# A two-layer spectral filter and token mixer: a list of the filter's steps put in another order, two loads issued later, a first step that takes its products in another order, and four matmuls that nothing reads

## Chip, cores and metric

One core of one Trainium2 chip. The metric is the device time of one launch in microseconds. The kernel before takes 997.96 us as the median of three runs (997.35 to 1001.58); its one profiled execution took 999.61 us.

## What is computed

The input x has 2048 tokens (S) of 640 channels (D), in fp32. Two layers alternate, each with a layer norm ahead of it and a residual sum behind it, and the pair runs twice:

```
def _A_ref(x, w_r, w_i):
    X = rfft2(x, axes=(-2, -1)) * (w_r + 1j * w_i)
    return irfft2(X, s=(S, D), axes=(-2, -1))

def _B_ref(x, w1, b1, w2, b2):          # token mixer, F = 1728
    u = gelu(einsum("bsd,sf->bdf", _layernorm(x), w1) + b1)
    return transpose(einsum("bdf,fs->bds", u, w2) + b2)

x = x + _A_ref(_layernorm(x), w_r, w_i)
x = x + _B_ref(_layernorm(x), w1, b1, w2, b2)
# ... and the same two lines once more
```

## The kernel before

**Number format.** Almost every matmul operand is an fp32 value carried as two fp16 tiles, a high part (names ending in h) and a low part (ending in l). A product of two such values is three matmuls: high by high, high by low, low by high (`mm3`, `prods`). Each intermediate is evicted from PSUM by a pair of instructions: ACT writes the high part, then DVE writes what is left as the low part.

**The filter layer.** The transform over 2048 tokens is done as 128 x 16, so there are 16 rows j of 128 tokens. In the row part (`a0_...`) each row is normalised, folded over the channels into f, and multiplied by a table tM into `s1h`/`s1l`. In the first layer that is done with fp32 f straight from x. In the second layer it is done while the token mixer before it ends, except for the last row j = 15, which `a0_tail` takes by itself: 11 matmuls that nothing reads (`WARM`) keep PE at work while DVE, POOL and ACT normalise the row (tiles eo, ft0, ft1, then fht and flt). Then come the row's products (from fht and flt into two PSUM tiles) and their eviction: s1h on ACT, s1l on DVE.

The middle part is `a1`. It goes over 16 groups g of frequencies, each in these steps:

- `d` (`dstage`, PE): products of s1h and s1l with the table tD into a PSUM tile. Groups 0 and 1 take 48 matmuls each (8 places in the PSUM tile, of 6 terms each: s1h twice and s1l once from one part, and the same from another). Groups from 2 take three terms for each place from s1h and s1l directly, and a fourth from `stk`, a tile that `stack` gathers for two groups at a time out of a DRAM copy (`rest`) of s1h and s1l: five DMAs of 64 or 0.5 KB for each pair of groups.
- `ph`, `pl`: eviction by ACT (high) and DVE (low).
- `sA`, `sB` (PE): the two halves of the next transform, from ph and pl with the table tS2. Here `acted` and `follow` add a synchronisation by hand: the last matmul of sA is waited for by an ACT instruction, and the first of sB waits for that ACT instruction. In the kernel before it is the first ACT step that stands behind sA in the list.
- `ta`, `tb` (DVE): the PSUM result times the filter's real and imaginary weight, both from the tile w of that group.
- `sa`, `sb` (POOL): the sums of these products. `xh` (ACT) and `xl` (POOL) split them, `uh` and `ul` (ACT) copy some columns.
- `i` (PE) and `Yh`, `Yl` (ACT, DVE): the transform back over one axis and its eviction.

**What sets the order.** `a1` runs these steps from a list, `STEPS`, written as text and the same for both layers. Every engine executes its instructions in the order in which they were issued in the program, so the list fixes each engine's own order. Besides, the list decides where DMA issues fall. After each op, `a1` tests whether ta and tb of group g-3 are already issued; if so it issues the load of w of group g (`wload`, 321 KB, three buffers), and likewise `stack` for the next pair of groups once the d steps of the pair three earlier are issued. Both go to the SP queue, which issues in order: an issue that must wait for a buffer to be released holds all issues behind it. SP also brings the token mixer's weights (`raw`, 512 KB) for the stage that comes later. POOL issues three DMAs of the first stk, and two larger loads for the part behind `a1`: `tDi` (966 KB) and `tIM0` (512 KB), both after sb3.

In the first layer `also` hangs further ACT and DVE work between the steps (finding scales and splitting the first block of the mixer's weights, tiles raw, junk and wh). It hangs on named ops, so it moves when they move in the list.

All of DVE's, ACT's, PE's and POOL's arithmetic is recorded through one helper, so its line is 69 for all of it (70 in the changed kernel). Lines of their own have the DMA issues: 494 and 496 stk, 506 w, 654 tDi, 655 tIM0, 895 raw.

Of the kernel before, what the change touches and what calls it, by code (L numbers as in the profile page):

```python
# [24 lines left out]
FIRST = 2  # L25
WARM = 11
STEPS = '''
    d1@1 sA0@2 ph1 pl1 sB0 d2@0 sA1@1 ph2 tb0 d3@3 ph3 sB1 ta0 sa0 pl2 sb0 xh0 xl0 sA2@0 tb1 uh0 pl3 d4@2 ta1 sa1 sb1
    sB2 ph4 ta2 sA3@3 d5@1 ul0 pl4 tb2 sB3 sb2 ph5 pl5 sA4@2 xh1 sa2 d6@0 d7@1 ta3 ph6 tb3 sB4 pl6 tb4 xl1 uh1 ph7
    sA5@3 xh2 i0@0 sb3 sB5 pl7 sa3 ta4 ul1 Yh0 Yl0 tb5 sA6@1 xl2 xh3 ta5 sb4 d8@2 ph8 d9@0 sa4 xl3 xh4 sB6 uh3 ul3 sa5  # L30
    pl8 tb6 sA7@3 uh2 sb5 i1@2 ph9 sB7 Yh1 xl4 ta6 pl9 d10@1 xh5 sb6 xl5 sA8@0 sa6 Yl1 ul2 ta7 ph10 i3@2 tb7 sB8 Yh3
    pl10 sA9@3 i2@1 ta8 uh4 sa7 xh6 ul5 tb8 sB9 Yl3 d11@0 ul4 sb7 Yh2 Yl2 xh7 xl6 uh6 sb8 sa8 uh5 sA10@2 tb9 ph11 xl7
    ta9 pl11 d12@1 xh8 sB10 sa9 ph12 sb9 i4@3 Yh4 i5@0 ta10 tb10 pl12 xh9 Yh5 xl8 d13@2 Yl4 sb10 ph13 sA11@1 ul6 Yl5
    uh8 pl13 sA12@3 sB11 sa10 ul7 xl9 xh10 xl10 sB12 ta11 tb11 ta12 sA13@2 d14@0 ph14 ul8 sa11 i6@1 sb11 ul9 Yh6 uh7
    sB13 tb12 pl14 Yl6 d15@3 xh11 sa12 uh9 sA14@0 tb13 sb12 ph15 xl11 i7@1 sB14 ta13 pl15 uh10 i8@2 ul10 uh11 xh12
    sa13 Yh7 sb13 i9@3 ul11 xh13 uh13 tb14 ta14 xl12 Yl7 sa14 uh12 Yh9 sA15@0 Yh8 sb14 Yl9 xh14 xl13 i10@1 sB15 i11@3
    Yh10 ul13 Yl8 xl14 i13@2 Yh11 uh14 tb15a ta15a ul14 ul12 sb15a Yh13 tb15b sa15a ta15b Yl10 Yl11 i14@0 Yl13 xh15a
    sb15b i12@1 sa15b xl15a xh15b uh15 xl15b i15a@2 Yh14 Yh12 Yl14 Yl12 ul15 Yh15a i15b@3 Yh15b Yl15a Yl15b
'''
SEQ = [t + 7 * i for t in (6, 0, 1, 2, 3, 4, 5) for i in range(2)]  # L40
EPS = 1e-5
# [35 lines left out]
class Layers:  # L77
# [367 lines left out]
    def a1(self, first):  # L445
# [68 lines left out]

        def dstage(g, ps):
            part = lambda t: tuple(s[:, t * 16 + g].rearrange("p h a b -> p (h a b)") for s in (self.s1h, self.s1l))
            for c, bk, o0, o1, k in CL:
# [19 lines left out]
        def xhi(g, c, x):  # L537

            return T.activation(xs[g % NX][0][:, :, c], x, AF.Copy)
# [74 lines left out]
        dst, half, waiting = {}, {}, []  # L614
# [13 lines left out]
        def acted(ins):  # L628

            for g in waiting:  # L630
                follow(ins, half[g])
                half[g] = ins
            waiting.clear()

        def do(op):

            name, g, c, dve, k = re.fullmatch(r"([a-zABY]+)(\d+)([ab]?)(!?)(?:@(\d))?", op).groups()
            g, W, ps = int(g), V if dve else G, slots[int(k or 0)]
            pair = lambda: (tt[g][0], tt[g][1])
            if name == "d":  # L640
                dst[g] = psplit(dstage(g, ps))
            elif name == "ph":
                acted(next(dst[g]))
            elif name == "pl":
                pp[g] = next(dst.pop(g))
            elif name in ("ta", "tb"):
                term(g, name == "tb", part[c])
            elif name == "sa":
                suma(pair(), part[c], W)
            elif name == "sb":  # L650
                ins = sumb(pair(), part[c], W)
                if g == 3:
                    with self.after(ins):
                        nc.gpsimd.dma_start(self.tDi, A["tDi"])
                        nc.gpsimd.dma_start(self.tIM0, A["tIM"][:, 0:4])
            elif name == "xh":
                acted(xhi(g, part[c], tt[g][0][:, :, part[c]]))
            elif name == "xl":
                xlo(g, part[c], tt[g][0][:, :, part[c]], W)
            elif name in ("uh", "ul"):  # L660
                acted(twice(g, name == "ul"))
            elif name == "sA":
                ps2[g] = ps
                half[g] = s2half(g, ps, pp[g], 0)[1]
                waiting.append(g)
            elif name == "sB":
                follow(s2half(g, ps2[g], pp.pop(g), 1)[0], half.pop(g))
            elif name == "i":
                pv[g, c] = ps
                for lt in range(3)[ltile[c]]:  # L670
                    is2mm(ps, g, lt)
            elif name == "Yh":
                acted(yhi(g, pv[g, c], ltile[c]))
            elif name == "Yl":
                ylo(g, pv[g, c], ltile[c])

# [37 lines left out]
        for op in STEPS.split():  # L714
            do(op)
            if first:
                also(op)
            ended.add(op.split("@")[0])
# [1305 lines left out]
```

## Time and profile before

| what | us |
|---|---|
| timed runs, median (lowest, highest) | 997.96 (997.35, 1001.58) |
| profiled execution, its own time | 999.61 |
| its span in the trace | 997.8 |
| time around the span (999.61 - 997.8) | 1.8 |
| PE busy | 949.3 (95%) |
| DVE busy | 774.9 (78%) |
| ACT busy | 575.1 (58%) |
| POOL busy | 302.1 (30%) |
| first filter's `a1` | 60.2 to about 124.7 |
| last row (`a0_tail`) before the second filter | about 548 to 555 |
| second filter's `a1` | 554.6 to about 622.5 |

Times in the trace are microseconds from the start of the span. PE's busy time includes matmuls that run at a lower granted clock, so a busy PE isn't always at the same speed; the row of granted clock (PEclk) has to be read beside it. A view by windows gives, for a stretch of time, PE's busy time with the number of instructions, the granted clock as a share of the full one, the DMA engines' busy share and GB/s.

### The profile page before, as it was taken

What the parts mean: (1) busy time and instruction counts of PE and PEld (TensorE: products, weight loads), DVE (VectorE), ACT (ScalarE), POOL (GpSimd) and SP (SyncE); (2) the same over time, 40 slices, a digit from 0 to 9 for tenths busy, and PEclk for the clock granted to TensorE, in tenths of its full rate; (3) what the DMA queues carried; (4) which work ended last, traced back from release to release, by engine and by line L of the source; (5) the groups of instructions that cost most, each with busy time, mean ns of one, the idle gap of its engine ahead of it and who ended that gap; (6) DMA issues with size and microseconds to landing.
All of it is one profiled execution on the core that took longest, in us unless ns stands there. A gap on an engine that the chain in (4) does not pass through costs nothing.

```text
span 997.8 us, 22816 instructions
## 1 busy us (share of the span) xinstructions
PE 949.3 (95%) x9126; PEld 703.5 (71%) x9126; DVE 774.9 (78%) x1488; ACT 575.1 (58%) x888; POOL 302.1 (30%) x512
## 2 busy tenths in 40 slices
PE   3879999999999999999999888999999999999998
PEld 2767777677776777777777666776777777677776
DVE  7979989988677884666666779789955666998885
ACT  4857859698656565555544457684644445454431
POOL 6939857322112102222222388583000000000000
PEclk9589999999999999999999999999999999999999
DMA  7856357657667655464431564574555447655411
GB/s 231 279 176 205 98 196 240 221 211 271 216 231 238 207 161 201 127 215 127 129 107 51 174 190 130 166 235 167 169 169 159 138 143 258 218 173 196 146 48 51
DMA packets 67454, 176.30 MB, mean 177 GB/s; under 512 B 8122, under 2 KB 15444, under 8 KB 67348
## 3 DMA queue, kind: packets, MB, share of 16 engines
q1 hardware_dynamic: 59380, 146.39, 46.2%
q0 software_dynamic: 7968, 28.46, 7.6%
q8 instruction: 71, 1.16, 0.5%
q14 instruction: 35, 0.29, 0.1%
HBM read 127.24 MB, written 47.58 MB: 175 GB/s over the span
## 4 chain that ended last, share of the span: by engine, by line
PE 61%; DVE 14%; issue 10%; DMA 5%; ACT 5%; POOL 4%; SPq 0%; POOLq 0%; DVEq 0%; ACTq 0%
PE ps L69 61%; DVE st L69 2%; DVE f L69 2%; DVE xt L69 1%; DMA w1S<-sp 1%; DVE s1l L69 1%; DMA raw<-w2z 1%; DVE hl L69 1%; DMA xt<-x 1%; POOL xt L69 1%; DVE Yl L69 1%; DVE wl L69 1%; DMA w<-w 1%; POOL w1A L935 1%; DVE S L69 1%
## 5 line engine op out<-in xcount | busy, mean ns | idle before, releaser
L69 PEld LDWEIGHTS <-wh 128*128 128x128 f16 x2602 | 251.5, 98 | 101.0 <-issue 2.4
L69 PEld LDWEIGHTS <-wl 128*128 128x128 f16 x1610 | 157.4, 98 | 63.2 <-DVE wl L69 1.3
L69 PE MATMUL ps<-ul,wh 128*128 128x320 f16 x448 | 133.0, 299 | 0.0
L69 PE MATMUL ps<-uh,wl 128*128 128x320 f16 x448 | 133.1, 299 | 0.0
L69 PE MATMUL ps<-uh,wh 128*128 128x320 f16 x416 | 124.3, 299 | 0.0
L69 PE MATMUL ps<-hl,wh 128*128 128x320 f16 x496 | 102.2, 299 | 0.8 <-DVE hl L69 0.8
L69 PEld LDWEIGHTS <-wo 128*128 128x128 f16 x756 | 73.9, 98 | 29.4 <-DVE wo L69 0.8
L69 DVE SCALAR_TENSOR_TENSOR wl<-raw,s,wh 128x896 f16<-128x896 f32 (+2 forms) x63 | 73.8, 1175 | 23.7 <-ACT wh L69 21.7
L69 POOL TENSOR_TENSOR r<-v,mh 128x1 f32<-128x1 f32 x64 | 37.3, 583 | 158.4 <-DVE nm L69 148.8
L69 ACT ACTIVATE junk<-raw 128x896 bf16<-128x896 f32 (+1 forms) x60 | 59.5, 992 | 32.0 <-DMA raw<-w 28.8
L69 PE MATMUL ps<-tDi,Yh 128*128 128x322 f16 x320 | 71.3, 300 | 0.4 <-ACT Yh L69 0.3
L69 ACT ACTIVATE wh<-raw,s 128x896 f16<-128x896 f32 (+2 forms) x66 | 66.5, 1032 | 5.5 <-DVE s L69 4.9
L69 DVE TENSOR_TENSOR f<-eo 128x256 f32<-128x256 f32 (+1 forms) x124 | 39.0, 367 | 37.8 <-POOL eo L69 37.0
L69 POOL TENSOR_TENSOR xt<-xt,ec 128x320 f32<-128x320 f32 x64 | 53.2, 853 | 32.7 <-DVE xt L69 32.6
L69 ACT ACTIVATE z<-xt,nb,r 128x640 f32<-128x640 f32 x31 | 28.5, 919 | 54.2 <-POOL z L69 43.1
L69 PE MATMUL ps<-u,wo 128*128 128x320 f16 x420 | 59.0, 299 | 0.5 <-DVE wo L69 0.5
L69 DVE BATCH_NORM_STATS2 st<-xt 128x6 f32<-128x320 f32 x126 | 55.2, 479 | 5.3 <-DMA xt<-x 4.7
L69 PE MATMUL ps<-hha,wh 128*128 128x320 f16 x288 | 58.1, 299 | 0.9 <-DVE wh L69 0.9
L69 PE MATMUL ps<-tM,f 128*128 128x128 f32 x160 | 37.6, 402 | 21.7 <-DVE f L69 21.6
L69 POOL TENSOR_TENSOR eo<-z 128x320 f32<-128x320 f32 x60 | 52.2, 891 | 17.2 <-ACT z L69 15.2
L69 PE MATMUL ps<-tDi,Yl 128*128 128x322 f16 x192 | 55.7, 299 | 1.4 <-DVE Yl L69 1.4
L69 PE MATMUL ps<-hha,wl 128*128 128x320 f16 x256 | 53.4, 299 | 1.0 <-DVE wl L69 1.0
(254 smaller groups left out, 2335.5 us busy)
## 6 DMA issues: line engine op xcount, KB each, us to landing
xt<-x SPq DMA_DIRECT2D x79, 320.0 KB
raw<-w SPq DMA_DIRECT2D x32, 512.0 KB
w<-w SPq DMA_DIRECT2D x48, 321.0 KB
x<-xt SPq DMA_DIRECT2D x47, 320.0 KB
raw<-w SPq DMA_DIRECT2D x32, 448.0 KB
raw<-w2z SPq DMA_DIRECT2D x32, 448.0 KB
w1S<-sp POOLq DMA_DIRECT2D x20, 512.0 KB, 3.9
out<-xt SPq DMA_DIRECT2D x15, 320.0 KB
```

Of the source, the lines that this page charges most:

```text
L69: i = f(*a, **k)
L935: (self.nc.sync if k else self.nc.gpsimd).dma_start(st[:, i], w[i][:, c * q:c * q + q])
```

## The change

Five edits:

1. `STEPS` is written in another order. Each engine's own sequence of the list's steps is unchanged on PE, ACT, DVE and POOL, and so are the pairs of sA and the ACT step that waits for it, which the list now names itself (`ph1&0`: ph1 waits for sA0). What moves is everything that the list triggers by where an op stands: the loads on SP, and the extra ACT work of the first layer.
2. `tDi` is loaded in two halves, after sb7 and after sb9, and `tIM0` after sb11, instead of both after sb3.
3. `dstage(0)` issues the products of s1h for all eight places first (32 matmuls), then those of s1l (16). The start and stop flags follow. This holds for both layers.
4. In `a0_tail`, so before the second filter alone, two matmuls of 128x512 that nothing reads stand behind the first two products of fht, and two more behind the row's last product. They write a PSUM half that nothing reads.
5. `mm3` is written out in `a0_tail` for edit 4; the products themselves stay.

The diff, cut:

```
 STEPS = '''
-    d1@1 sA0@2 ph1 pl1 sB0 d2@0 sA1@1 ph2 tb0 d3@3 ph3 sB1 ta0 sa0 pl2 sb0 xh0 xl0 sA2@0 tb1 uh0 pl3 d4@2 ta1 sa1 sb1
...
+    d1@1 sA0@2 ph1&0 pl1 sB0 d2@0 tb0 ta0 sA1@1 d3@3 ph2&1 sa0 sb0 pl2 sB1 ph3 sA2@0 tb1 xh0 d4@2 uh0&2 pl3 xl0 ta1
...
+        def fill(n):
+            for _ in range(n):
+                self.PE.matmul(warm[:, 1], m[:, 0, 0], self.tD.rearrange("p a b -> p (a b)")[:, :512], start=True, stop=True)
...
-                self.mm3(q[:, c], (fh[:, c], fl[:, c]), (m[:, j % 4, 0], m[:, j % 4, 1]), True, True)
+                a, b = (fh[:, c], fl[:, c]), m[:, j % 4]
+                self.PE.matmul(q[:, c], a[0], b[:, 0], start=True, stop=False)
+                self.PE.matmul(q[:, c], a[0], b[:, 1], start=False, stop=False)
+                if not i and not o:
+                    fill(2)
+                self.PE.matmul(q[:, c], a[1], b[:, 0], start=False, stop=True)
             qs.append((q.rearrange("p (a h b) -> p a h b", h=2, b=4), slice(64 * i, 64 * i + n // 8)))
+        fill(2)
...
-                for i, (a, b) in enumerate(terms):
-                    for o, f in zip(HALF, HALF[::-1] if bk else HALF):
-                        mm(ps[o, bk, o0:o1], a[:, f], b, start=i == 0, stop=i == len(terms) - 1)
+                todo.append((bk, o0, o1, terms))
+            whole = [(slice(0, 6),)] if g else [(slice(0, 2), slice(3, 5)), (slice(2, 3), slice(5, 6))]
+            for cut in whole:
+                for bk, o0, o1, terms in todo:
+                    some = sum((terms[c] for c in cut), [])
+                    for i, (a, b) in enumerate(some):
+                        for o, f in zip(HALF, HALF[::-1] if bk else HALF):
+                            mm(
+                                ps[o, bk, o0:o1], a[:, f], b, start=cut is whole[0] and i == 0 and (g > 0 or o0 == 0),
+                                stop=cut is whole[-1] and i == len(some) - 1 and (g > 0 or o0 > 0),
+                            )
...
-                if g == 3:
+                if g in (7, 9, 11):
                     with self.after(ins):
-                        nc.gpsimd.dma_start(self.tDi, A["tDi"])
-                        nc.gpsimd.dma_start(self.tIM0, A["tIM"][:, 0:4])
+                        if g < 11:
+                            nc.gpsimd.dma_start(self.tDi[:, g // 9], A["tDi"][:, g // 9])
+                        else:
+                            nc.gpsimd.dma_start(self.tIM0, A["tIM"][:, 0:4])
```

Three places in the engines' order show what moves. The first is SP's queue in the second filter, before. In it w_1094 is the load of group 5, w_1102 that of group 6, w_1107 of group 7 and w_1110 of group 8; stk_1097 is the gathered tile of groups 12 and 13.

```order
L506 DMA w_1094_8776<-w 128x642
L494 DMA stk_1097_8873<-rest0_12_1063_8375 32x4x256
L496 DMA stk_1097_8873<-rest0_12_1063_8375 1x256
L494 DMA stk_1097_8873<-rest0_12_1063_8375 32x4x256
L494 DMA stk_1097_8873<-rest1_12_1063_8376 32x4x256
L496 DMA stk_1097_8873<-rest1_12_1063_8376 1x256
L506 DMA w_1102_8886<-w 128x642
L506 DMA w_1107_8976<-w 128x642
L506 DMA w_1110_9000<-w 128x642
```

And the same stretch in the changed kernel, where stk_1098 is the tile of groups 12 and 13, w_1113 the load of group 8, and raw_1179 a block of the mixer's weights:

```order
L518 DMA w_1094_8793<-w 128x642
L518 DMA w_1102_8892<-w 128x642
L506 DMA stk_1098_8880<-rest0_12_1063_8380 32x4x256
L508 DMA stk_1098_8880<-rest0_12_1063_8380 1x256
L506 DMA stk_1098_8880<-rest0_12_1063_8380 32x4x256
L506 DMA stk_1098_8880<-rest1_12_1063_8381 32x4x256
L508 DMA stk_1098_8880<-rest1_12_1063_8381 1x256
L518 DMA w_1107_8981<-w 128x642
L916 DMA raw_1179_10421<-w1 128x1024
L518 DMA w_1113_9078<-w 128x642
```

The load of group 6 has moved ahead of the five DMAs of stk; the load of raw_1179, which stood some rows further ahead (in front of the tile of groups 10 and 11), now stands behind the load of group 7.

The second place is PE at the end of `a0_tail` and the start of d0 of the second filter. Before, the row's last product (flt1) is followed by d0, which goes from four products of s1h to two of s1l in each place of the PSUM tile:

```order
L69 LDWEIGHTS flt1_1059_8317
L69 MATMUL ps1060_8333<-tM3_708_5780,flt1_1059_8317 128x128
L69 LDWEIGHTS s1h707_5769
L69 MATMUL ps1070_8395<-tD707_5771,s1h707_5769 64x160
...
L69 LDWEIGHTS s1l707_5770
L69 MATMUL ps1070_8395<-tD707_5771,s1l707_5770 64x160
```

In the changed kernel two of the unread matmuls (into ps1048, from tD and tM3) stand between the row's last product and d0, and d0 goes on with s1h:

```order
L70 LDWEIGHTS flt1_1059_8318
L70 MATMUL ps1060_8336<-tM3_708_5781,flt1_1059_8318 128x128
L70 LDWEIGHTS tM3_708_5781
L70 MATMUL ps1048_8283<-tD707_5772,tM3_708_5781 128x512
...
L70 LDWEIGHTS s1h707_5770
L70 MATMUL ps1070_8400<-tD707_5772,s1h707_5770 64x160
...
L70 MATMUL ps1070_8400<-tD707_5772,s1h707_5770 64x161
```

The first product of s1l stands behind 32 products of s1h now, and behind 4 before.

The third place is POOL in the first filter, before (the second filter's order is the same). The rows of ta are the sums sa and sb, from the products ta and tb; ta_255 is group 3:

```order
L69 TENSOR_TENSOR xl1_219_881<-ta_244_1231,xh1_219_880 128x2x321
L69 TENSOR_TENSOR ta_255_1411<-tb_258_1416,ta_255_1411 128x321
L654 DMA tDi218_874<-tDi 128x3864
L655 DMA tIM0218_873<-tIM 128x1024
L69 TENSOR_TENSOR ta_255_1411<-ta_255_1411,tb_258_1416 128x321
L69 TENSOR_TENSOR xl2_219_883<-ta_248_1252,xh2_219_882 128x2x321
```

In the changed kernel, where ta_282 is group 7 and ta_295 group 9:

```order
L70 TENSOR_TENSOR ta_282_1764<-tb_285_1807,ta_282_1764 128x321
L675 DMA tDi218_874<-tDi 128x1932
L70 TENSOR_TENSOR xl1_219_881<-ta_280_1697,xh1_219_880 128x2x321
...
L70 TENSOR_TENSOR ta_295_2004<-tb_292_1964,ta_295_2004 128x321
L675 DMA tDi218_874<-tDi 128x1932
L70 TENSOR_TENSOR xl3_219_885<-ta_288_1842,xh3_219_884 128x2x321
```

POOL's two issues behind the sums of group 3 are gone, and three issues stand behind those of groups 7, 9 and 11 (the last one, of tIM0, is not in these rows).

More of the change, by code (lines that the diff above doesn't have):

```diff
@@ new lines @@
+    tb7 sa6 sB8 pl10 Yh3 sA9@3 sa7 ta8 i2@1 uh4&9 sb7 xh6 tb8 ul5 sB9 ul4 xl6 Yl3 Yh2 d11@0 xh7 Yl2 sb8 uh6 sA10@2 uh5
+    tb9 sa8 d12@1 ph11&10 xl7 ta9 xh8 sB10 pl11 ph12 i4@3 sa9 ta10 sb9 i5@0 tb10 Yh4 xl8 pl12 xh9 d13@2 Yh5 Yl4 sb10
+    sA11@1 ph13 Yl5 sa10 sA12@3 ul6&11 xl9 uh8 pl13 sB11 ul7&12 xh10 sB12 ta11 sA13@2 xl10 d14@0 tb11 ta12 sa11 i6@1
+    ph14&13 tb12 sb11 ul8 ul9 sB13 pl14 Yh6 sa12 d15@3 uh7 sb12 Yl6 xh11 uh9 sA14@0 tb13 xl11 i7@1 ph15&14 ta13 uh10
+    ul10 sB14 pl15 uh11 xh12 sa13 i8@2 tb14 Yh7 sb13 i9@3 ta14 ul11 xl12 xh13 Yl7 uh13 sA15@0 uh12 Yh9 sa14 i10@1
@@ L39 @@
+    Yh8&15 sb14 Yl9 xl13 xh14 sB15 Yl8 i11@3 Yh10 tb15a xl14 ul13 ta15a i13@2 Yh11 tb15b uh14 sb15a ta15b ul14 Yl10
+    ul12 i14@0 Yh13 sa15a sb15b Yl11 xh15a sa15b i12@1 xh15b uh15 xl15a Yl13 Yh14 Yh12 Yl14 xl15b i15a@2 ul15 Yl12
+    i15b@3 Yh15a Yh15b Yl15a Yl15b
 '''
@@ L613, in a1 @@
         slots = [self.big() for _ in range(4)]
-        dst, half, waiting = {}, {}, []
+        dst, half = {}, {}
         tt = collections.defaultdict(dict)
@@ L626, in a1, with acted @@
             V.scalar_tensor_tensor(c, a, sc, b, op0=ALU.mult, op1=ALU.subtract)
-        def acted(ins):
-            for g in waiting:
+        def acted(ins, gs):
+            for g in map(int, gs.split(",") if gs else ()):
                 follow(ins, half[g])
                 half[g] = ins
-            waiting.clear()
         def do(op):
-            name, g, c, dve, k = re.fullmatch(r"([a-zABY]+)(\d+)([ab]?)(!?)(?:@(\d))?", op).groups()
+            name, g, c, dve, k, f = re.fullmatch(r"([a-zABY]+)(\d+)([ab]?)(!?)(?:@(\d))?(?:&([\d,]+))?", op).groups()
             g, W, ps = int(g), V if dve else G, slots[int(k or 0)]
@@ L642, in do @@
             elif name == "ph":
-                acted(next(dst[g]))
+                acted(next(dst[g]), f)
             elif name == "pl":
@@ L651, in do @@
                 ins = sumb(pair(), part[c], W)
-                if g == 3:
+                if g in (7, 9, 11):
                     with self.after(ins):
-                        nc.gpsimd.dma_start(self.tDi, A["tDi"])
-                        nc.gpsimd.dma_start(self.tIM0, A["tIM"][:, 0:4])
+                        if g < 11:
+                            nc.gpsimd.dma_start(self.tDi[:, g // 9], A["tDi"][:, g // 9])
+                        else:
+                            nc.gpsimd.dma_start(self.tIM0, A["tIM"][:, 0:4])
             elif name == "xh":
-                acted(xhi(g, part[c], tt[g][0][:, :, part[c]]))
+                acted(xhi(g, part[c], tt[g][0][:, :, part[c]]), f)
             elif name == "xl":
@@ L660, in do @@
             elif name in ("uh", "ul"):
-                acted(twice(g, name == "ul"))
+                acted(twice(g, name == "ul"), f)
             elif name == "sA":
@@ L717, in a1 @@
                 also(op)
-            ended.add(op.split("@")[0])
+            ended.add(re.match(r"\w+", op).group())
             if wn < NG and {f"ta{wn - 3}", f"tb{wn - 3}"} <= ended:
```

17 lines of the change are left out of this document (5 added, 12 removed).

## The prediction, made before the changed kernel ran

> **What bounds the kernel now.** I read the page first: the busy shares and the span in 40 slices.
>
> ```profile
> PE 949.3 (95%) x9126; PEld 703.5 (71%) x9126; DVE 774.9 (78%) x1488; ACT 575.1 (58%) x888; POOL 302.1 (30%) x512
> PE   3879999999999999999999888999999999999998
> ```
>
> PE is busy for 95% of the span, so the kernel can gain only where PE waits or runs slowly. A slice is 24.9 us. Slices 22 to 24 (548 to 623 us) show 8 in the PE row: this is the second filter. The first filter lies in slices 2 to 4. The change touches nothing outside these two stretches, so I read only them, next along the chain of work that ended last:
>
> ```profile
> 576.92 7.30 DMA w<-w
> ...
> 584.34 0.20 DVE tb L69
> ...
> 586.07 14.04 PE ps L69 x344
> ```
>
> A filter weight w is issued at 576.92 and lands 7.30 us later, and everything waits for it. DVE's own rows show what the wait costs (the bracket is idle time before the row, with its releaser):
>
> ```profile
> 572.97 0.88 DVE L69 SCALAR_TENSOR_TENSOR tb<-ps,sx,w 128x642 f32<-128x642 f32 x1
> ...
> 579.48 0.82 DVE L69 SCALAR_TENSOR_TENSOR pl<-ps,ph 128x642 f16<-128x642 f32 x1
> 584.34 0.89 DVE L69 SCALAR_TENSOR_TENSOR tb<-ps,sx,w 128x642 f32<-128x642 f32 x1 [4.04 <-DMA w<-w]
> ...
> 587.60 0.88 DVE L69 SCALAR_TENSOR_TENSOR ta<-ps,sx,w 128x642 f32<-128x642 f32 x1
> ...
> 590.37 0.83 DVE L69 SCALAR_TENSOR_TENSOR pl<-ps,ph 128x642 f16<-128x642 f32 x1 [1.11 <-ACT ph L69]
> ```
>
> DVE had finished pl of group 8 at 579.48 + 0.82 = 580.30 and stood until 584.34 for group 6's weight. Then the view by windows, cut to PE's clock steps (columns: stretch, its length and PE's busy time in it with the number of instructions, granted clock, DMA share, GB/s):
>
> ```profile
> 551.94:555.35 3.41, 1.82 (x21) 0.99 0.00 0
> 555.35:558.76 3.41, 3.26 (x50) 0.51 0.89 284
> ...
> 579.24:582.66 3.42, 2.82 (x78) 1.00 1.13 350
> 582.66:586.07 3.41, 0.00 (x0) 0.99 0.62 191
> 586.07:589.48 3.41, 3.41 (x50) 0.51 0.36 101
> ```
>
> The wait costs twice. PE does nothing from 582.66 to 586.07, and in the next 3.41 us its granted clock is 0.51. The same pair stands at 551.94 and 555.35: a window with PE busy for 1.82 of 3.41, then one at half the clock. In the first filter it is 2.03, and near the second filter's end 2.17, which is not followed by a slow one:
>
> ```profile
> 53.59:57.01 3.42, 2.03 (x13) 0.99 0.76 198
> 57.01:60.42 3.41, 2.62 (x14) 0.50 0.77 257
> ...
> 609.96:613.38 3.42, 2.17 (x65) 1.00 0.69 257
> 613.38:616.79 3.41, 3.41 (x109) 1.00 0.03 9
> ```
>
> So in this trace a window of 3.41 us with PE busy up to 2.03 us is followed by one at half the clock, and with 2.17 it is not.
>
> **A, the stall at 582 us.** SP's rows say why the weight was late:
>
> ```profile
> 572.63 0.35 SPq L506 DMA_DIRECT2D w<-w  x1
> 573.75 0.30 SPq L494 DMA_DIRECT2D stk<-rest  x1
> ...
> 576.92 3.00 SPq L506 DMA_DIRECT2D w<-w  x3
> ```
>
> Group 5's weight goes out at 572.63, then five stk issues come, the first waiting until 573.75, and only at 576.92 group 6's. By then the two loads that POOL issues are in flight ahead of it:
>
> ```profile
> 574.76 0.57 POOL L654 DMA_DIRECT2D tDi<-tDi  x1
> 575.32 0.56 POOL L655 DMA_DIRECT2D tIM<-tIM  x1
> ...
> tDi<-tDi POOLq DMA_DIRECT2D x1, 966.0 KB, 5.9
> ...
> tIM<-tIM POOLq DMA_DIRECT2D x1, 512.0 KB, 7.0
> ```
>
> 966 + 512 = 1478 KB stand before 321 KB. The change takes away both reasons: group 6's load is right behind group 5's, and POOL's loads come after groups 7, 9 and 11. The load still waits for its buffer, group 3's, which is free once tb of that group ends: 572.97 + 0.88 = 573.85. So it goes out at about 573.9. How long it then takes is bounded from this trace by 7.30 (the slow load above) and by the first w of the first filter, in its own chain:
>
> ```profile
> 58.08 2.73 DMA w<-w
> ```
>
> With 2.73 it lands at 576.6, with 7.30 at 581.2, against a need at 580.3. I take 2.73, since the 1478 KB are no longer ahead; even twice that lands at 579.4, in time. The worst end gives 4.04 - 0.9 = 3.1 us back, the other all 4.04. With no empty window there is no slow one: its 3.41 us hold 3.41 x 0.51 = 1.74 us of work at full clock, so 1.67 more, 5.7 in all. What is late next is DVE, which has its own work for each group (3.26 us from the products of group 6 at 584.34 to those of group 7 at 587.60): it can give back only the time in which it idled, 4.04 + 1.11 = 5.15. I take 5.2.
>
> Something goes back on POOL. In the second filter's later part it has no room:
>
> ```profile
> 592.61:608.15 15.54, 15.43 (x16) 1.00 0.46 125
> ```
>
> It is busy for 15.43 of 15.54 us. Two issues of 0.57 leave the stretch ahead of the stall and three (1.7) come into or just before this one. If all three delay the end, it is 1.7; if the two that go were themselves in the way it is up to 0.4 better than now. I take the difference of one issue, 0.6. A is -5.2 + 0.6 = **-4.6** (from -6.1 to -1.4).
>
> **B, the first filter.** Two waits of PE are touched:
>
> ```profile
> 60.17 0.48 PE L69 MATMUL ps<-tD,s1h 128*64 128x160 f16 x4 [0.79 <-ACT s1h L69]
> 61.03 0.35 PE L69 MATMUL ps<-tD,s1l 128*64 128x160 f16 x2 [0.38 <-DVE s1l L69]
> ...
> 89.08 0.33 PE L69 MATMUL ps<-ph,tS 64*64 64x321 f16 x4 [0.76 <-ACT xh L69]
> ```
>
> In d0, 32 products of s1h now stand before the first of s1l, and not 4. A row of four takes 0.48 here; even if seven more overlap by half they last 1.7 us, far above the 0.38 of the second row's wait: -0.4. At 89.08 PE waits for an ACT step behind the extra scan of a raw tile:
>
> ```profile
> 87.70 1.04 ACT L69 ACTIVATE junk<-raw 128x1024 bf16<-128x1024 f32 x1
> ```
>
> The new list puts this scan at other places among ACT's steps, and POOL's two issues (1.13 us) leave the stretch just before. The trace doesn't show the new order's waits; between the whole 0.76 won and 0.6 lost (the scan standing in another step's way) I take 0.5 won, since the scan's 1.04 is the nearest row and covers the wait. B is **-0.9** (from -1.2 to +0.2).
>
> **C, the start of the second filter.** PE's rows:
>
> ```profile
> 549.70 2.54 PE L69 MATMUL ps<-tD,tM 128*128 128x512 f16 x11
> ...
> 553.17 0.23 PE L69 MATMUL ps<-tM,flt 128*128 128x128 f16 x1 [0.50 <-DVE flt L69]
> ...
> 554.59 0.33 PE L69 MATMUL ps<-tD,s1h 128*64 128x160 f16 x4 [0.52 <-ACT s1h L69]
> 555.50 0.35 PE L69 MATMUL ps<-tD,s1l 128*64 128x160 f16 x2 [0.57 <-DVE s1l L69]
> ```
>
> The three waits make up most of what the window from 551.94 lacks. Four unread matmuls (the eleven earlier ones take 2.54 us, so 0.23 each) add 0.9 us, and s1h's products fill the third wait. The window rises from 1.82 to 2.7 or more, above 2.17, and d0 runs at full clock. In the chain its last 44 products are one piece:
>
> ```profile
> 555.50 3.18 PE ps L69 x44
> ```
>
> At 0.51 that is 1.62 us of work, so d0 would last from 554.59 to about 556.3 and not to 558.7. The fills cost nothing, as they end inside waits on DVE and ACT that remain. But the 2.4 us do not reach the end, since the next step is bound by a load (POOL's issue, the times to landing of stk between 553 and 566, and the first use):
>
> ```profile
> 558.15 0.57 POOL L494 DMA_DIRECT2D stk<-rest  x1
> ...
> DMA to landing us min/median/max: 3.8/4.2/4.7
> ...
> 562.97 0.24 PE L69 MATMUL ps<-tD,stk 96*64 96x160 f16 x2
> ```
>
> The first stk is gathered from the finished s1h and s1l, whose time the change leaves alone. It lands 3.8 to 4.2 us after 558.15, at about 562.0 to 562.4, and d2 uses it at 562.97 now: at most 0.8 can be won. That use stands 4.3 us behind d0's end; with d0 done at 556.3 PE would be there at 560.6 and wait 1.4 to 1.8 us. Together with the waits on ACT and DVE that these 4.3 us hold already, a window of 3.41 us up to 562 would have PE busy for less than 2. By the rows above that brings a half-clock window at 562, costing up to 1.7; whether a window falls so is open. -0.8 to +0.9; I take **0**.
>
> The Trainium skill bears on this place: "TensorE: Matmul & The Clock Gate", section "Why this matters for your kernels", says that the drop is avoided as long as PE has no idle gaps over about 3 us. By it the fills would be useless and the thin stretch up to 562 harmless, so C would be the gain alone; the trace disagrees at 555.35, where waits of 0.50, 0.52 and 0.57 us were followed by the clock 0.51.
>
> **Sum.** A -4.6, B -0.9, C 0: -5.5. The profiled execution took 999.61, 1.65 above the median of 997.96. So 999.61 - 5.5 = 994.1 for a like execution, and **992.5** as median. 0.5%, or 5.0 us, is about what a measurement of this kernel can tell from no change: faster means below 993.0, slower above 1002.9.
>
> **Rivals.**
> 1. *Part of it is given back in the same filter.* d2 starves and the half clock comes at 562 (C at +0.9), and POOL's three issues are all late at the end (A at -3.5): 997.96 - 3.5 - 0.9 + 0.9 = 994.5, or 995.6 with B at +0.2. For it: POOL's 15.43 of 15.54, and the 1.4 to 1.8 us before d2. Against it: a POOL that starts its full stretch 4 us sooner also ends it sooner. Chance 0.25.
> 2. *The weight is late all the same.* Another issue holds it: w of group 6 waits for a buffer, or later ones wait behind raw, which now stands between groups 7 and 8. Then only B remains: 997. Against it: group 8 is used two groups, or 6.5 us, behind group 6. Chance 0.08.
> 3. *Slower: the stall moves to a later weight.* tDi's halves now meet the loads of groups 10 to 12, in both filters. If such a load takes over 6.5 us, two groups of DVE's work (2 x 3.26), as the one at 576.92 did with 7.30, DVE stands again. The second filter then keeps its cost, and the first, which has no such stall today, gains one of 4.0 + 1.7: 997.96 + 5.7 - 0.4 = 1003.3. Against it: a half is 483 KB, not 1478 at once. Chance 0.07.
> 4. *Short gaps don't slow the clock.* Only gaps longer than any before 555.35 would. Then 562 is harmless and C is -0.8 in full: 992.5 - 0.8 = 991.7. Against it: the windows above. Chance 0.12.
>
> **Chances.** My forecast has 0.48. Its own spread and rival 4 lie about 992.5, so roughly two thirds of them are below 993.0; with a little of rival 1: faster 0.45, within 0.5% 0.48, slower 0.07. The range takes the sum's bounds at the low end, -6.1 - 1.2 - 0.8 = -8.1, or 989.9, and reaches to rivals 1 and 2 at the high end: 989.9 to 997.0.
>
> **Signs.** Right: DVE's tb of group 6 has no wait on w, SP issues w of groups 5 and 6 together, no empty PE window and no half clock from 575 to 600; no half clock right after the last row, but PE waiting for stk before d2; POOL full to the end; no s1l wait in either d0. Wrong: a half-clock window anywhere from 575, a DVE wait on w after tDi's issues, or a first filter that is longer than before.

## The result, and the profile after

The changed kernel takes 998.31 us as the median of 12 runs (993.17 to 999.92), the kernel before 998.65 us beside it (996.25 to 1001.58): a ratio of 0.999, 95% interval 0.9974 to 1.0006. That is no difference, where 992.5 was forecast. The profiled execution took 998.46 us with a span of 996.7, against 999.61 and 997.8.

The stall at 582 us is gone. DVE's rows of the changed kernel at that place (columns as before):

```profile
583.15 0.82 DVE L70 SCALAR_TENSOR_TENSOR pl<-ps,ph 128x642 f16<-128x642 f32 x1
583.90 0.89 DVE L70 SCALAR_TENSOR_TENSOR tb<-ps,sx,w 128x642 f32<-128x642 f32 x1
...
588.74 0.82 DVE L70 SCALAR_TENSOR_TENSOR pl<-ps,ph 128x642 f16<-128x642 f32 x1
```

They follow each other without a wait on w, and no half-clock window comes behind them. But the same tb of group 6 starts at 583.90 against 584.34 before: 4 us of wait are gone, and it is 0.44 us earlier. The rest was lost ahead of it. The view by windows of the changed kernel, from the last row's tail on, cut to its clock steps:

```profile
552.39:555.80 3.41, 2.65 (x37) 1.00 0.00 0
555.80:559.22 3.42, 2.98 (x88) 1.00 0.52 181
559.22:562.63 3.41, 1.51 (x30) 1.00 0.96 269
562.63:566.05 3.42, 1.24 (x20) 0.50 0.58 165
566.05:569.46 3.41, 3.41 (x52) 0.50 0.45 126
...
579.70:583.11 3.41, 3.30 (x90) 1.00 0.73 224
583.11:586.53 3.42, 3.42 (x99) 1.00 0.84 274
```

d0 now runs at full clock, as forecast (552.39 to 559.22). Then comes a window with PE busy for 1.51 of 3.41 us, and behind it two at half clock, not none or one (the first of them holds 1.24 us of work). PE's row says what it waits for, the chain how long:

```profile
564.81 0.35 PE L70 MATMUL ps<-tD,stk 96*64 96x160 f16 x2 [3.28 <-DMA stk<-rest]
```
```profile
560.72 4.00 DMA stk<-rest
564.72 0.09 issue
564.81 10.36 PE ps L70 x206
```

The first stk lands at 564.72; 562.0 to 562.4 was forecast. It still takes 4.00 us, but POOL issues its last part at 560.72, not at 558.15. POOL's rows, before and then after, with what it waited for:

```profile
557.01 0.64 POOL L494 DMA_DIRECT2D stk<-rest  x1 [6.64 <-DVE wl L69]
```
```profile
559.58 0.64 POOL L506 DMA_DIRECT2D stk<-rest  x1 [9.26 <-DMA rest<-s1l]
```

POOL starts 2.57 us later. The profile names s1l's copies in the row after and a DVE step in the row before, but in the program the three stk issues of POOL read one copy alone: the small one of s1h into `rest` (64 KB), SP's first issue. The trace's semaphore records bear that out. The copy lands in sixteen parts, and POOL's first issue comes 0.75 to 0.76 us behind the last part, before, after and in every kernel below. Counted from DVE's last step on zt (at 548.23 before, 548.18 after), the fifteenth part lands at 7.99 before and 8.62 after, the sixteenth at 8.02 and 10.64. So the whole copy is 0.6 late, and one part of it another 2.0.

The 0.6 comes from ACT's eviction of s1h, before and after:

```profile
553.94 0.77 ACT L69 ACTIVATE s1h<-ps 128x512 f16<-128x512 f32 x2 [1.32 <-PE ps L69]
```
```profile
554.49 0.77 ACT L70 ACTIVATE s1h<-ps 128x512 f16<-128x512 f32 x2 [1.92 <-PE ps L70]
```

It waits 0.60 longer for PE: this is the second pair of unread matmuls (553.86 to 554.45). The one late part has its like in SP's issues of the copies:

```profile
554.73 0.80 SPq L501 DMA_DIRECT2D rest<-s1h  x2
555.66 0.86 SPq L501 DMA_DIRECT2D rest<-s1l  x2
```
```profile
555.28 0.80 SPq L513 DMA_DIRECT2D rest<-s1h  x2
556.17 2.32 SPq L513 DMA_DIRECT2D rest<-s1l  x2
```

The two issues of s1l, which stand behind those of s1h, take 2.32 us in place of 0.86. In the stretch of the copies, the DMA view of the changed kernel has one packet of a queue that the kernel doesn't program, "instruction":

```profile
q8 instruction: 1, 0.02, 3.5%
```

By the trace's packets it is 16 KB at 556.15 and takes 1.5 us of one of the 16 DMA engines (the trace doesn't say which), which fits a copy with one late part in sixteen. The kernel before has such a packet too, but at 557.69, when the small copy of s1h has landed (556.25). There the sixteenth part of the small copy of s1l is the late one (11.46, the fifteenth 9.53), and POOL doesn't wait for it. There are 71 of them in both kernels, 16.4 KB each, against 18,252 PE instructions with weight loads (2 x 9,126): one for every 256 instructions of 64 bytes, if they are PE's. So this is taken as the fetch of PE's next instructions; the experiments bear it out, since PE instructions that are added ahead of it move it.

DVE executes the same instructions in the same order in both kernels, so the difference between equal steps shows where time went. The last step on zt starts at 548.23 before and 548.18 after, so this pair of traces shows no gain from the first filter there (B). tb of group 1 starts at 566.46 before and 570.40 after: 4.0 us lost at the front (C). By Yl at the filter's end

```profile
612.11 1.95 DVE L69 SCALAR_TENSOR_TENSOR Yl<-ps,Yh 128x384 f16<-128x384 f32 x4 [0.39 <-ACT Yh L69]
```
```profile
611.29 1.95 DVE L70 SCALAR_TENSOR_TENSOR Yl<-ps,Yh 128x384 f16<-128x384 f32 x4 [0.89 <-ACT Yh L70]
```

the changed kernel is 0.82 ahead: 4.76 us won after the front (A).

### The profile page after: what moved, and what is told of

It is laid out like the page before. It is cut to its first block, busy times and chain, and to the rows that moved or that the text cites. A ratio compares the mean times of both kernels' runs of the same rounds, so it can differ in the third digit from the quotient of the medians.

```text
span 996.7 us, 22831 instructions
## 1 busy us (share of the span) xinstructions
PE 948.7 (95%) x9130; PEld 701.2 (70%) x9130; DVE 774.9 (78%) x1488; ACT 575.0 (58%) x888; POOL 302.9 (30%) x514
## 4 chain that ended last, share of the span: by engine, by line
PE 52%; DVE 21%; ACT 9%; POOL 7%; DMA 6%; issue 5%; SPq 0%; ACTq 0%; DVEq 0%; POOLq 0%
PE ps L70 52%; DVE wl L70 3%; DMA xt<-x 3%; POOL eo L70 3%; DVE st L70 3%; DVE f L70 3%; DVE xt L70 2%; ACT z L70 2%; DVE s1l L70 1%; POOL xt L70 1%; ACT wh L70 1%; DVE hl L70 1%; ACT xt L70 1%; DMA w<-w 1%; ACT junk L70 1%
```

## Experiments

All ratios are to runs of the kernel before on the same chip, so they don't follow from the medians, which come from several chips; each kernel has 6 to 12 runs. In the table, times are microseconds from the start of DVE's last step on zt in each trace (548.23 before, 548.18 after; the expectations call it the tail's start), read from the rows of ACT, POOL and PE and from the packets of the instruction queue. The column "filter" is the time from that step to the end of the second filter's last Yl, in the one profiled run. SP issues the four copies from 6.5 to 8.3, or from 7.1 to 8.9 where s1h is late.

| kernel | instruction packet | ACT s1h | POOL's first stk | PE's first use of stk | filter | median | ratio (95%) |
|---|---|---|---|---|---|---|---|
| before | 9.46 | 5.71 | 8.78 | 14.74 | 74.61 | 997.82 to 998.65 | 1 |
| changed | 7.96 | 6.31 | 11.39 | 16.63 | 73.56 | 998.31 | 0.999 (0.9974 to 1.0006) |
| e1_no_fill2 | 7.49 | 5.72 | 11.21 | 16.30 | 72.42 | 994.26 | 0.9958 (0.9941 to 0.9974) |
| e2_no_fills | 8.42 | 5.72 | 8.79 | 14.23 | 68.59 | 994.91 | 0.9966 (0.9947 to 0.9985) |
| e3_shift_fetch | 3.62 | 6.31 | 9.38 | 15.52 | 71.87 | 992.57 | 0.9939 (0.992 to 0.9959) |
| e4_other_tile | 7.88 | 5.71 | 10.65 | 15.84 | 72.91 | 996.60 | 0.9989 (0.9973 to 1.0005) |
| f1_shift_other_tile | 4.00 | 5.71 | 8.89 | 13.49 | 67.51 | 991.61 | 0.9935 (0.9916 to 0.9954) |
| f2_stk_last | 3.52 | 5.70 | 8.88 | 15.18 | 68.77 | 989.13 | 0.9908 (0.989 to 0.9927) |
| f3_list_and_loads | 9.41 | 5.71 | 8.77 | 14.07 | 71.01 | 992.84 | 0.9959 (0.994 to 0.9979) |
| f4_before_shift | 6.03 | 5.71 | 9.01 | 13.65 | 74.22 | 997.54 | 0.9994 (0.9978 to 1.001) |
| g1_fetch_hit | 6.37 | 5.72 | 9.18 | 13.86 | 68.92 | 991.19 | 0.993 (0.9905 to 0.9955) |
| g2_list_only | 9.49 | 5.71 | 8.77 | 14.12 | 72.49 | 998.54 | 1.0006 (0.9988 to 1.0024) |
| g3_loads_only | 9.45 | 5.71 | 8.76 | 14.02 | 69.19 | 992.68 | 0.995 (0.9933 to 0.9967) |
| g4_stk_last | 9.36 | 5.71 | 8.77 | 14.19 | 68.17 | 992.38 | 0.9944 (0.9926 to 0.9962) |
| h1_fetch_8 | 7.24 | 5.71 | 10.26 | 15.54 | 71.31 | 995.54 | 0.9977 (0.9959 to 0.9996) |
| h2_fetch_12 | 7.54 | 5.72 | 10.91 | 16.34 | 71.08 | 996.49 | 0.9976 (0.9961 to 0.9991) |
| h3_fills_only | 8.04 | 6.31 | 10.98 | 16.19 | 77.17 | 1000.83 | 1.0033 (1.0014 to 1.0051) |
| h4_d0_order_only | 7.56 | 5.71 | 10.96 | 16.36 | 75.62 | 998.08 | 0.9993 (0.9977 to 1.001) |

**What delays the front.** e1 takes one line out of the changed kernel:

```
-        fill(2)
         for q in ps:
             self.a0_s1l(*q)
```

> The changed kernel without the second pair of unread matmuls (those behind the row's last product). Theory T1: that pair writes the PSUM tile from which ACT takes s1h, so ACT waits for it (s1h from 553.94 before to 554.49), and the copies of s1h, the first stk and d2 follow. Then s1h starts within 0.1 us of the kernel before (553.9), the copies go out 0.55 earlier, d2's wait for stk falls from 3.28 to 2 us or less, and the time is 2 to 4 us under the changed kernel (994 to 996). Theory T2 (the 16 KB fetch of PE's instructions among the copies of s1h decides alone): s1h is 0.5 earlier, but stk lands only that much earlier, unless the fetch falls elsewhere; 997.5 to 998. Theory T3 (a d0 at full clock only moves the wait to d2, whatever s1h does): d2 waits for 2.5 us or more, half clock follows, 997 to 998.5.

s1h is on time again (5.72), and the ratio falls from 0.999 to 0.9958 (about 3 us). But POOL is only 0.18 earlier: the instruction packet lies among the copies, and the copy's last part lands at 10.46. T1 holds for s1h only; the median falls where T1 had it, though d2 still waits (3.54 us in its profile, then one half-clock window, not two).

e2 takes out both pairs.

> The changed kernel without all four unread matmuls; the order of d0's products, the list and the later loads stay. T1: s1h as before the change (553.9), the window before d0 is thin again, d0 runs at half clock, the first stk lands at 562 as before, d2 does not wait over 0.5 us, and the gain of the stall at 582 us shows: 993 to 994.5. T2: 993 to 995 as well if the fetch comes behind the copies as in the kernel before, 997.5 if it does not. T3: like T1, 993 to 994.5, since d0 is slow again. Against all: if it stays at 997.5 or more, the stall at 582 was worth nothing.

The packet comes behind the copies, POOL is on time, and 994.91 shows part of the gain; the runs spread from 989.94 to 999.24. In the profiled run d0 was at full clock without the unread matmuls. So a full clock there doesn't need them in every run.

e3 changes only how the warm-up is cut, which adds 66 PE instructions at the same PE time:

```
-        for _ in range(WARM):
-            self.PE.matmul(warm[:, 0], ..., ...[:, :512], start=True, stop=True)
+        for _ in range(4 * WARM):
+            self.PE.matmul(warm[:, 0, :128], ..., ...[:, :128], start=True, stop=True)
```

> The changed kernel with its 11 unread warm-up matmuls of 512 columns as 44 of 128 columns: the same PE time within 0.3 us, but 66 more PE instructions, which puts PE's next fetch of 256 instructions ahead of the last row's end. T1: s1h still starts 0.55 late, no fetch lies among the copies; stk lands about 0.6 late in place of 2.7, at 562.6, d2 waits 1.2 us; 995 to 996.5. T2: stk lands at 562 to 562.6 and all of the loss behind the fetch is back: 994.5 to 996. T3: d2 still waits over 2.5 us, 997.5 to 998.5.

With the packet gone from the copies, POOL starts at 9.38, which is 8.78 plus the 0.60 of the late s1h and nothing else, and the ratio falls from 0.999 to 0.9939 (about 5 us; T1 and T2 had less). SP's and POOL's rows of that kernel:

```profile
556.88 0.90 SPq L513 DMA_DIRECT2D rest<-s1l  x2
```
```profile
558.26 0.64 POOL L506 DMA_DIRECT2D stk<-rest  x1 [7.24 <-DVE wl L70]
```

The issues take 0.90 again, and all sixteen parts of the copy have landed by 8.62. The profiled run was the slowest of six (997.5) and still has a wait of 2.17 us at d2, so its own time says little.

e4 writes the second pair into the row's other PSUM tile (`fill(2, own)` with `own` the tile of the last product).

> The changed kernel with the second pair of unread matmuls written into the other PSUM tile of the row (the one of its last 128 columns), whose eviction comes second. PE's work is that of the changed kernel. T1: s1h of the first tile starts at 553.9, like without the pair; the copies go out 0.3 to 0.55 earlier than in the changed kernel; 994 to 997. T2: nothing changes for the fetch, 997 to 998.5. T3: 997.5 to 998.5. If s1h still starts at 554.5, the pair delays it in another way than by the tile (it stands in PE's queue between product and signal).

With the same PE work s1h starts at 5.71: it was the shared tile that made ACT wait, and not PE's queue. The packet still meets the copies, and the time stays near the changed kernel's.

f1 has both mends; f2 besides issues the stk products of d2 and d3 last:

```
+            late = g in (0, 2, 3)
...
+            elif late:
+                whole = [(slice(0, 3),), (slice(3, 4),)]
```

> The changed kernel with both mends together: 44 warm-up matmuls of 128 columns in place of 11 of 512 (so that no fetch of PE's instructions falls among the copies of s1h), and the second unread pair written into the other PSUM tile (so that ACT's s1h does not wait for it). Theory T1+fetch (both delays are separate and add): POOL issues the first stk 8.8 us after DVE's row xt copy that opens the tail, as in the kernel before (8.78), against 11.39 in the changed one, 9.38 with the shift alone and 10.65 with the other tile alone; d2 reaches its stk at 14.9 or earlier (16.63 in the changed kernel); time 991 to 993.5. Rival (only the fetch counts): like the shift alone, 992 to 993.5, POOL at 9.4. Rival (d2 waits on something else): 994 or more.

> As the kernel with both mends, and d2 and d3 issue their products of s1h and s1l for all places first and those of stk last (24, then 8), as d0 does with s1l. If d2's wait for stk is what limits the start of the filter, 0.85 us of products (18 more ahead of the wait) are hidden in it, and PE is less thin before: 0.5 to 1.5 us better than without, 990 to 992.5. Rival (after the mends d2's wait is no longer on the path): no difference within 1 us.

Both delays are gone from f1 (5.71, 8.89), and it is at 991.61. f2, at 989.13, is the fastest kernel here, 2.5 us below f1 where 0.5 to 1.5 were expected (the two intervals touch), with all six runs from 988.72 to 990.78. Its first use of stk stands later in the program, behind 24 products, so its column isn't comparable (nor is g4's). In the profiles its second filter is not shorter than f1's (68.77 against 67.51), so where the 2.5 us come from is not shown. In its profile PEclk shows no slice at half clock:

```profile
PEclk9999999999999999999999999999999999999999
```

The profile of g1, which has neither edit 3 nor edit 4, has the same row, so it is not the mark of f2's edits.

**The instruction packet by itself.** f4, g1, h1 and h2 change only how the warm-up is cut, in the kernel before (f4: 36 more PE instructions) or in f3 (18, 8 and 12 more). Like e3's edit, for instance in h1 (4 matmuls of 512 columns as 8 of 256):

```
-        for _ in range(WARM):
+        for _ in range(WARM - 4):
             ...
+        for _ in range(8):
+            self.PE.matmul(warm[:, 0, :256], ..., ...[:, :256], start=True, stop=True)
```

> The kernel before with 6 of its 11 unread warm-up matmuls of 512 columns as 24 of 128: the same PE time, 36 more PE instructions, nothing else. If a fetch of PE's instructions among the copies of s1h delays the first stk by itself, the fetch moves from 9.46 us behind the tail's start to about 8, POOL's first stk issue from 8.78 to 10.5 or later, and d2 waits 1.5 us or more for stk; the time is 0.5 to 2.5 us above before, less than the delay since the stall at 582 takes part of it. Rival (the fetch only accompanies an earlier d0 and delays nothing): stk stays at 8.8, the time as before within 1 us.

> The list and the later loads alone (992.84 so far), with 3 of the 11 unread warm-up matmuls of 512 columns as 12 of 128: the same PE time, 18 more PE instructions. Theory (a fetch of PE's instructions among the copies of s1h delays the first stk): with no such instructions the fetch stood 9.41 us behind the tail's start, with 36 more at 6.03 in another kernel, so 18 put it at 7.3 to 8.2, among the copies (6.5 to 8.3). POOL's first stk issue moves from 8.77 to 10.5 or later, d2 reaches its stk 1 to 2.5 us later, a half clock follows, and the time is 1.5 to 3.5 us longer: 994.5 to 996.5. Rival (the fetch only accompanies other changes and delays nothing): POOL stays at 8.8 and the time at 992 to 993.5.

> The list and the later loads alone, with 4 of the 11 unread warm-up matmuls of 512 columns as 8 of 256: the same PE time, 8 more PE instructions. With none more the fetch of PE's instructions stood 9.41 us behind the tail's start, with 18 more at 6.37. Theory (a fetch among the copies of s1h delays the first stk by itself): if the fetch falls at 7.2 to 8.2, POOL's first stk issue goes from 8.77 to 10.5 to 11.4, d2 reaches its stk 1 to 2.5 us later than 14.07, and the median is 1 to 3 us above 992.8. Rival: a fetch at 7.2 to 8.2 with POOL still at 8.8 to 9.2. If the fetch falls elsewhere this run says nothing on it.

> As the run with 8 more PE instructions, but 12 more (6 of the warm-up matmuls as 12 of 256). Same theories: fetch at 7.2 to 8.2 and POOL's first stk at 10.5 or later with a median of 994 to 996, or POOL unmoved at 8.8 to 9.2 and 992 to 993.5.

f4 and g1 missed: the packet jumped to 6.0 and 6.4, ahead of the copies, and POOL moved by 0.2 to 0.4 only. h1 and h2 hit. (In h2's POOL row below, the profile again names s1l's copy.) The DMA view over the copies and the issues of f3, then of h2:

```profile
q1 hardware_dynamic: 433, 0.56, 60.2%
```
```profile
556.51 0.85 SPq L510 DMA_DIRECT2D rest<-s1l  x2
```
```profile
q1 hardware_dynamic: 271, 0.43, 43.7%
q8 instruction: 1, 0.02, 3.7%
```
```profile
554.93 2.51 SPq L512 DMA_DIRECT2D rest<-s1l  x2
```
```profile
558.40 0.64 POOL L505 DMA_DIRECT2D stk<-rest  x1 [8.77 <-DMA rest<-s1l]
```

With 12 more PE instructions of the same total PE time, one instruction packet lies among the copies, their issue takes 2.51 in place of 0.85, and POOL starts 2.1 us later than in f3; with 8 more, 1.5 us. In both, the fifteenth part of s1h's small copy lands at 8.02, as in f3, and the sixteenth at 10.16 and 9.50. The times follow: g1, the same arithmetic with the packet ahead of the copies, has 0.993 (0.9905 to 0.9955), h1 0.9977 (0.9959 to 0.9996) and h2 0.9976 (0.9961 to 0.9991). That is 4 to 5 us between g1 and these two, whose intervals lie apart from its own; f3's 0.9959 lies between, and its interval overlaps with theirs. The second filter took 71.31 and 71.08 us in the profiles of h1 and h2, 68.92 in that of g1 and 71.01 in that of f3, which has two half-clock windows from 609 us on. So the delay of stk is shown, and its price is known to a few us only. In the table, every kernel whose packet starts between 7.2 and 8.1 has POOL 1.5 to 2.4 us late beyond the 0.60 of a late s1h, and no other has over 0.4. In each of the late ones it is the sixteenth part of the copy that is late; the fifteenth is on time (8.02 to 8.13, or 8.62 behind a late s1h).

**What the parts give alone.** f3 takes edits 3 and 4 out of the change; g2 has the new list alone; g3 the later loads alone; h3 the unread matmuls alone; h4 d0's order alone. g4 is f3 with stk last.

```
g3, all of it:
-                if g == 3:
+                if g in (7, 9, 11):
                     with self.after(ins):
-                        nc.gpsimd.dma_start(self.tDi, A["tDi"])
-                        nc.gpsimd.dma_start(self.tIM0, A["tIM"][:, 0:4])
+                        ... (as in the change)
h4, all of it: dstage as in the change
h3, all of it: a0_tail as in the change
```

> The kernel before with the new list and the later loads alone: no unread matmuls in the tail, d0 in its old order. Theory: step A of the prediction was right in size (group 6's weight no longer waits, -4.6 in the second filter), and the first filter gains something: the time from the tail's start to the filter's end is 4 to 5.5 us shorter than before, and the whole 992.5 to 994.5. Rival: the stall at 582 was covered by something else, 996.5 to 998.

> The kernel before with the new list alone. On SP the load of group 6 still stands behind the five stk issues here, and POOL issues its two large loads after group 3 as before. Theory (the stall at 582 comes from these two loads ahead of the weight): the stall of 4 us and the half clock behind it stay, the whole is within 1.5 us of before, 996.5 to 998. Rival (the list frees it in another way): 994 or less.

> The kernel before with the later tDi and tIM0 alone. On SP the load of group 6 still stands behind the five stk issues and goes out at about 576.9. Theory (the two large loads ahead of it were what made it late): it takes 2.7 to 3.4 us in place of 7.3, lands before or about when DVE needs it (580.3), and most of the gain is there: 993 to 995. Rival (the place in SP's queue made it late): the wait stays at 2 us or more, 996 to 998.

> The kernel before with the four unread matmuls alone (edit 4). Theory (the second pair holds ACT's s1h by its PSUM tile): s1h starts 6.3 us behind the tail's start in place of 5.7, and everything behind it in the filter is 0.6 later, with another 2 if the fetch of PE's instructions falls among the copies of s1h; the stall at 582 takes up a part: 998 to 1000. Rival (the matmuls cost nothing and save a half-clock window, as the prediction had it): 996.5 to 998.

> The kernel before with the new order of d0's products alone (edit 3). In its SP queue the load of group 6 stands ahead of the five stk issues, and tDi and tIM0 are still issued after group 3. Theory 1 (the two large loads, not the place in SP's queue, made the weight late): the weight goes out at about 574, just ahead of them or with them, takes 4 us or more and the stall shrinks to 0 to 2.5 us; 994 to 997. Theory 2 (the place alone is enough): no wait on the weight, 992.5 to 994. Theory 3 (neither): the wait stays at 4 us, 997 to 998.5.

> The list and the later loads, with d2 and d3 issuing their stk products last, but no unread matmuls in the tail, d0 in its old order and the warm-up as before. If the early d0 and the unread matmuls give something by themselves once their two delays are mended (989.13 with them), this is slower, at 991 to 993; if all of the gain beyond 992.84 comes from stk last, it is at 988.5 to 990.

The list gives nothing (998.54), the loads alone all of it (992.68), and f3 with both is no better (992.84). In g2 two waits on a weight stay, 1.20 us on group 5's and 3.36 on group 6's; in g3 the one on group 6's is down to 0.15 us, though SP issues this weight as late as before, at 575.31 behind the five stk. DVE's rows, g2 and then g3:

```profile
583.24 0.89 DVE L70 SCALAR_TENSOR_TENSOR tb<-ps,sx,w 128x642 f32<-128x642 f32 x1 [3.36 <-DMA w<-w]
```
```profile
579.04 0.89 DVE L69 SCALAR_TENSOR_TENSOR tb<-ps,sx,w 128x642 f32<-128x642 f32 x1 [0.15 <-DMA w<-w]
```

h4 shows the other half. There the load of group 6 does stand ahead of the stk issues, with tDi and tIM0 as before, and the wait moves to group 7's weight:

```profile
592.97 0.89 DVE L69 SCALAR_TENSOR_TENSOR ta<-ps,sx,w 128x642 f32<-128x642 f32 x1 [2.89 <-DMA w<-w]
```

So it was the 1478 KB, not the place in SP's queue. h4's median also carries the instruction packet (7.56), so its 998.08, in the range of the third theory, is not the price of the place alone. The unread matmuls alone make the kernel slower (h3, 1.0033, so 3.3 us): late s1h and the packet together. g4 is not told apart from f3: stk last gives nothing measurable there. It is slower than f2 (0.9908), with intervals that touch, as its first expectation had it; but f1, with edits 3 and 4 and both mends, is not told apart from f3, g3 and g4, which lack these edits. So a gain of edits 3 and 4 once they are mended is possible and not shown. Several medians lie outside the range of the theory that the traces bear out: e3 and g3 below it, e2, g2, h2, h3 and h4 above, by 0.3 to 1.9 us, which is less than the runs of one kernel spread.

## Why the prediction was wrong

- **A, the stall: right in size, partly wrong in cause.** -4.6 was forecast; 4.76 us are won behind the front in the trace, and f3 and g3 are 4.1 and 5.0 us below before by their ratios. The sum of 4.04, the half-clock window and the 1.11 bound by DVE held as a whole. Its terms were not measured one by one: the 0.6 given back on POOL is untested, and group 6's load took 4.53 us in the changed kernel and 3.61 in g3 where 2.73 was taken, and was in time or 0.15 late all the same. That the sum comes within 0.2 us is in part luck. "The change takes away both reasons" did not: only the later loads count. The order of SP's queue, which the step put down to the list, is that of before in f3 and g2 and the new one in h4: it comes with d0's order.
- **B, the first filter: not confirmed, and too small for these runs.** -0.9 was forecast. Both waits are gone in the profile (in d0 the products of s1l follow those of s1h directly, and the 0.76 at 89.08 is no longer there), and the first filter's last Yl ends 1.49 us earlier (124.58 against 126.07). At DVE's step on zt 0.05 of that is left. Neither number can be put down to the edits: f4 has the first filter of before and ends it at 123.63, and the stretch from there to zt, whose program no edit changes, took 420.47 to 426.14 us in the 18 profiles. The list alone measures 1.0006 (0.9988 to 1.0024). So nothing shows the 0.9, and nothing excludes it.
- **C, the front of the second filter: the step that failed.** 0 was forecast, with -0.8 to +0.9; it is +4.0. The window went above the limit and d0 ran at full clock, as the step had it (though it did so without edits 3 and 4 too, in f3 and g1 to g4). Two of its sentences were wrong: "The fills cost nothing, as they end inside waits on DVE and ACT that remain", and the first stk "is gathered from the finished s1h and s1l, whose time the change leaves alone". The second pair shares a PSUM tile with the product that ACT reads, which makes s1h 0.60 late (e4). And the earlier and longer run of PE instructions brings the next instruction packet among the copies of s1h, so that one part in sixteen of the small copy lands another 2.0 later, and POOL waits for it (e3, h1, h2). Together POOL's first stk is 2.6 us late, d2 waits 3.28 us, and two half-clock windows follow in place of the one at +0.9. Rival 1 had d2 starving and a half clock at 562, but not what makes stk late, and its price for C was +0.9.
- **Rival 4 and the clock.** The half clock followed a window with PE busy for 1.51 of 3.41 us, as the limit read from the rows before would have it. But that limit is no rule: in the changed kernel a window with 1.96 is followed by a half clock and one with 1.89 is not, and in g2 one with 1.58 is not, though PE waits 3.32 us from there into the next (rows below). The Trainium skill's rule ("TensorE: Matmul & The Clock Gate", "Why this matters for your kernels": no idle gaps over about 3 us) would have this half clock too, since the wait is 3.28 us. Against the rule speak the half clocks at 57.01 and 555.35 of before and at 67.70 of the changed kernel, behind gaps of at most 0.86 us, and g2's gap of 3.32 us without one. What sets the half clock off stays open.
- **Rivals 2 and 3** did not come: no weight is waited for after the loads at groups 7, 9 and 11.

The windows of the fourth bullet (columns as before), of the changed kernel and then of g2:

```profile
64.29:67.70 3.41, 1.96 (x36) 1.00 0.79 231
67.70:71.11 3.41, 3.41 (x50) 0.50 0.40 109
...
95.00:98.41 3.41, 1.89 (x50) 1.00 0.52 210
98.41:101.83 3.42, 3.42 (x108) 1.00 0.37 101
```
```profile
580.06:583.48 3.42, 1.58 (x48) 1.00 0.87 290
583.48:586.89 3.41, 1.92 (x48) 1.00 0.42 115
```

## What to carry to other kernels

An instruction that nobody reads is not free: it is in the way of whoever waits on the same tile, and it moves the instruction fetches behind it. A copy has landed only when its last part has: where a step waits for one, look at the last part, and not only at the name that the profile gives the wait. Where a chain of small copies feeds the next step, look whether a packet of the instruction queue falls among them before and after an edit, and try the same work in a few more or fewer instructions. And of two loads that seem to delay a third, take each away alone before either is named the cause.

## What was not expected of the hardware

- One 16 KB packet of the instruction queue, 0.9 to 1.8 us long, makes one part in sixteen of a small copy 1.5 to 2.4 us later than the other fifteen, and with it all that waits for the copy. With 8 or 12 more PE instructions at the same PE work it fell so (h1, h2), with 18 more it did not (g1): 0.9977 and 0.9976 against 0.993, and 0.9959 with none added (f3).
- The half clock after a thin stretch is not there in every run: d0 of the second filter ran at half clock in the profile of before and of h2, and at full clock in those of f3, g1, g2, g3 and g4, whose PE work there is that of before or nearly so. In f3 the windows of 3.41 us cut the same steps elsewhere: PE is busy for 2.67 and 2.31 us in the two from 551.44 on, where before has 1.82 and then the half clock.
- The runs of one kernel spread by up to 9.5 us (before, 992.65 to 1002.1), more than most of the edits are worth, and much of it arises where nothing was edited: 420.47 to 426.14 us between the two filters in these profiles.
